# Turning keys and probabilities in 32x32 blocks on VectorE instead of on TensorE, in a decode step of attention and a gated feed-forward

## The chip, the cores and the metric

The kernel runs on one core of one Trainium2 chip. The metric is the device time of one execution in microseconds (us), as the median of several runs. The core has a matrix engine (TensorE, PE in the profile, with its weight loads as PEld), a vector engine (VectorE, DVE), an activation engine (ScalarE, ACT), GpSimd (POOL) and SyncE (SP), which here only issues transfers. Each engine takes its instructions in the order of its own list and waits at semaphores for the others. Sixteen DMA engines move data between the off-chip memory and the on-chip memory of 128 partitions (SBUF). TensorE writes into PSUM, eight banks of 2 KB per partition.

## The reference

One token of a decode step for a batch of 8. A normalised x goes two ways: through grouped-query attention over the last 2048 entries of a key and value cache (32 query heads, 8 key heads, 128 wide), and through a gated feed-forward. The results are multiplied and added to x.

```python
xn = _layernorm(x)                                        # 8 x 512
q  = (xn @ wq) as 8 x 32 heads x 128                      # wq 512 x 4096
k, v = the last W = 2048 rows of the caches, 8 heads, each used by 4 query heads
p  = softmax(q k^T * 128 ** -0.5);  o = p v
s  = o as 8 x 4096 @ wo                                   # wo 4096 x 512
g  = silu((sigmoid(xn @ w_gate) * (xn @ w_up)) @ w_down)  # 512 x 1792, 1792 x 512
out = x + s * g
```

All data are bf16. The caches that are read are 8 batches x 8 heads x 2048 x 128 for keys and as much for values, 67 MB; the weights are another 14 MB.

## The kernel before

**Storage and transfers.** One tile `ring` holds nine slots of 16 KB per partition. A cache tile is one slot: four key heads of one batch, so that partition 4p + l holds 64 consecutive cache rows of head l of the four (`G` = 4, 32 partitions for each head). A batch has two key tiles and two value tiles (`i` = 0, 1). The list `todo` fixes the order of all loads: gate and up weights, the plain part of w_down, a slot for its gathered part, wq, then the keys of tile n with the values of tile n - 3, and wo at the end in four pieces. `pump` issues the next load of the list on SP's queue as soon as the list's head finds a free slot (L172 for cache tiles, L123 for weights); `free` gives a slot back after the last instruction that reads it. The slot of a key tile is given back in `k_transposes`, that of a value tile in `value`.

**The gather.** Of w_down, the first `m0` rows come by an indirect DMA from POOL's queue (L239): 64 partitions each get `SF` rows in one piece, the others none. `SEGS` lists which partitions these are; a selection matrix `sel` on TensorE spreads the matching part of the hidden vector to the same partitions. The remaining rows come as one plain load of `MT` rows per partition.

**Head.** Layer norm, gate and up products, transposes of the hidden vector, then the queries (L387): wq is 512 x 4096, four contraction steps by eight column blocks, written four at a time into the four 32-column strips of the array. Two groups of four transposes bring them into `qm_sb`, padded by zeros so that a window of 32 columns puts the four query rows of one head at the right place.

**Attention, per batch.** The code's main loop (from L675 on) runs over batches `b` and sixteen steps. In each step `k_transposes` turns eight blocks of 128 keys x 128 on TensorE through `perm` into PSUM (L484), and VectorE copies the 128x1024 result to SBUF (L489). After two steps `scores` (L502) forms four products of 32 rows x 512 keys, side by side in the array, into one PSUM bank per batch, whose 128 rows are head of the tile x eighth of the batch's keys (tile and quarter) x query. `row_max` takes each row's own maximum (L515) and four exponentials of 32 rows (L522), with the sums. As each row has a maximum of its own, `stat_rows`, `factor` and `spread` work out, in one row of 128 numbers on one partition, what each row must be scaled by. `p_transposes` turns the probabilities on TensorE (L591) and copies them (L596). `value` (L612) multiplies them by the values two batches behind, in 16 steps for each of the two value tiles; `combine` scales on ScalarE (L632), `normalise` and `turn` bring the result into the layout `oP_sb` (L642, L651, L660, L667). Up to batch 4 (`WIDE`) a value product has 64 rows and 512 columns, after that two of 32 rows and 256.

**Tail.** After the last keys the stages of the last batches are written out one by one, with filler products (`keep`) between them, then the output product with wo (`into`, L372, two halves of 64), two vector instructions (L756, L758) and two stores.

The order on each engine is the order of the code: there is no scheduler, and the tables of `tasks` are written out by hand.

Of the kernel before, what the change touches and what calls it, by code (L numbers as in the profile page):

```python
# [10 lines left out]
def kernel(  # L11
# [30 lines left out]
    CH = CU // 2  # L42
    NU = NQ * NJ
    NR = NU * rep
# [18 lines left out]
    ps_t = ctx.enter_context(  # L63
        tc.tile_pool(name="ps_t", bufs=4, space=bass.MemoryType.PSUM)
    )
    ps_s = ctx.enter_context(
        tc.tile_pool(name="ps_s", bufs=2, space=bass.MemoryType.PSUM)
# [68 lines left out]
    MT = 9  # L136
    SF = 10
    NSEL = 64
    SEGS = [(0, 15, 1), (16, 3, 1), (28, 18, 1), (48, 2, 1)]
    SEGS += [(60, 8, 1), (68, 6, 4), (92, 8, 1), (124, 4, 1)]  # L140
# [142 lines left out]
    xnT_sb = work.tile([P, KT, Z], bf16, name="xnT_sb")  # L283
    nc.vector.memzero(xnT_sb[:])
    nc.vector.tensor_copy(out=xnT_sb[:, :, :B], in_=xnT_ps[:])  # L285
# [8 lines left out]
    M0 = Z - rep  # L294
    qm_sb = work.tile([P, B, Hkv, M0 + Z], bf16, name="qm_sb")
    nc.gpsimd.memzero(qm_sb[:])
    p_buf = [work.tile([P, PG, G, CU], bf16, name=f"p_buf{i}") for i in range(2)]
    for t in p_buf:
        nc.gpsimd.memzero(t[:])
# [20 lines left out]
    for k in range(F // FC):  # L320
        g_ps = ps_t.tile([B, FC], f32, name="g_ps", tag="t")
        for kt in range(KT):
            nc.tensor.matmul(  # L323
                g_ps[:],
                lhsT=xnT_sb[:, kt, :B],
# [9 lines left out]
    h_bf = ktpool.tile([P, CU * P], bf16, name="h_bf", tag="kT")  # L335
    for k in range(F // FC):
        u_ps = ps_t.tile([B, FC], f32, name="u_ps", tag="t")
        for kt in range(KT):
            nc.tensor.matmul(  # L339
                u_ps[:],  # L340
                lhsT=xnT_sb[:, kt, :B],
# [40 lines left out]
    q_ps = [ps_t.tile([P, D], f32, name="q_ps", tag="t") for _ in range(2)]  # L382
    for kt in range(KT):
        for e in range(2):
            for g in range(G):
                c0 = (G * e + g) * D
                nc.tensor.matmul(  # L387
                    q_ps[e][Z * g : Z * (g + 1), :],
                    lhsT=xnT_sb[:, kt, :],
                    rhs=weights[("wq_sb", kt)][:, c0 : c0 + D],  # L390
                    start=(kt == 0),
                    stop=(kt == KT - 1),
                    tile_position=(0, Z * g),
                    skip_group_check=True,
                )
    free(rows_of[("wq_sb", 0)])
    spot_ps = ps_t.tile([P, SF, B], f32, name="spot_ps", tag="t")
# [14 lines left out]
    for e in range(2):  # L412
        q_bf = ktpool.tile([P, D], bf16, name="q_bf", tag="kT")
        nc.scalar.mul(out=q_bf[:], in_=q_ps[e][:], mul=scale)
# [187 lines left out]
    def value(b, i, c):  # L602
# [18 lines left out]
        if c == CU - 1:  # L621
            free(v_tiles.pop((b, i)))
# [173 lines left out]
```

## Time and profile before

| | |
|---|---|
| median of 3 runs | 198.41 us (198.28 to 198.48) |
| the profiled execution: its own time, its span | 198.86 us, 197.1 us |
| PE, DVE, ACT, POOL busy | 163.4, 125.7, 40.8, 9.1 us |
| DMA moved | 81.32 MB, mean 413 GB/s |
| DVE copies of turned keys (L489) | 128 x 684 ns = 84.3 us busy |
| PE transposes of keys (L484) | 1024, 73.4 us busy |
| PE score products (L502) | 256, 25.8 us busy |
| PE value products (L612) | 352, 36.6 us busy |
| chain that ended last, by engine | DMA 65%, PE 25%, DVE 5%, ACT 3% |

The span runs from the first to the last instruction; the execution's own time is 1.8 us longer. Busy time is the sum over instructions of an engine; matmuls overlap, so the mean duration of one is longer than its share of the stream. A line of the profile names the source line, the engine, what was written and read, and the count. The row "DMA" of the slices gives in tenths how full the sixteen DMA engines were in each fortieth of the span. A window's line has start and end, its length, the busy time and count of PE, PEld, DVE, ACT and POOL, the granted clock of TensorE as a share, the DMA share and GB/s.

### The profile page before, as it was taken

Reading aid. Unit: us, or ns where it says so; the run is one execution under the profiler, and the core shown is the slowest. Engines: PE = TensorE matmul, PEld = TensorE weight load, DVE = VectorE, ACT = ScalarE, POOL = GpSimd, SP = SyncE. Lnnn points to the kernel's source line nnn. Section 1 sums busy time; section 2 is a strip of 40 time slices with the busy share of each in tenths; the row PEclk is TensorE's granted clock in tenths of the full one; section 3 lists DMA queues with packets and bytes.
Section 4 is the critical chain, followed back from the end, with each engine's and each line's share of the span. In section 5 each row is a group of like instructions: output and inputs, shape, how many; then the busy total and the mean of one; then the engine's idle time right before and its main releaser. Section 6 shows DMA issues by size and latency. Waiting matters only on the chain.

```text
span 197.1 us, 4818 instructions
## 1 busy us (share of the span) xinstructions
PE 163.4 (83%) x2114; PEld 106.8 (54%) x2114; DVE 125.7 (64%) x247; ACT 40.8 (21%) x95; POOL 9.1 (5%) x31
## 2 busy tenths in 40 slices
PE   0029859999699999799979987999799998878883
PEld 0013423876576575456646654665467566655652
DVE  4540401999799796679667966796549878935201
ACT  0053003001701501600160016001600070071000
POOL 7910000000000000000000000000000000000000
PEclk9999966999999999999999999999879999999999
DMA  6999999999999999999999999999999999999990
GB/s 203 438 440 463 416 406 426 436 436 432 424 429 429 422 426 422 439 432 432 426 432 434 426 426 421 429 436 426 419 442 439 426 431 422 426 429 429 420 401 16
DMA packets 6148, 81.32 MB, mean 413 GB/s; under 512 B 808, under 2 KB 816, under 8 KB 1328
## 3 DMA queue, kind: packets, MB, share of 16 engines
q1 hardware_dynamic: 5936, 80.35, 96.0%
q0 software_dynamic: 144, 0.66, 0.8%
q8 instruction: 16, 0.26, 0.5%
q14 instruction: 4, 0.03, 0.0%
q10 hardware_dynamic: 48, 0.01, 0.0%
HBM read 81.67 MB, written 0.01 MB: 414 GB/s over the span
## 4 chain that ended last, share of the span: by engine, by line
DMA 65%; PE 25%; DVE 5%; ACT 3%; issue 1%; SPq 0%; ACTq 0%
DMA ring<-in_A_k_cache_dram 29%; DMA ring<-in_A_v_cache_dram 13%; PE kT_ps L484 13%; DMA ring<-in_A_wq_dram 11%; DMA ring<-in_A_wo_dram 10%; PE s_ps L502 4%; PE o_ps L612 3%; DMA ring<-in_B_w_gate_dram 3%; DVE kT_sb L489 2%; PE q_ps L387 2%; ACT p_buf L522 2%; PE fin_ps L372 1%; PE d_ps L403 1%; DVE pT_sb L596 1%; ACT L522 1%
## 5 line engine op out<-in xcount | busy, mean ns | idle before, releaser
L489 DVE COPY kT_sb<-kT_ps 128x1024 bf16<-128x1024 bf16 x128 | 84.3, 684 | 26.0 <-PE kT_ps L484 21.2
L484 PE MATMUL kT_ps<-perm,ring 128*128 128x128 bf16 x1024 | 73.4, 221 | 2.0 <-DMA ring<-in_A_k_cache_dram 2.0
L484 PEld LDWEIGHTS <-ring 128*128 128x128 bf16 x1024 | 59.5, 99 | 24.6 <-issue 18.3
L612 PE MATMUL o_ps<-ring,pT_sb 128*32 128x256 bf16 (+1 forms) x352 | 36.6, 330 | 6.6 <-DMA ring<-in_A_v_cache_dram 5.6
L502 PE MATMUL s_ps<-kT_sb,qm_sb 128*32 128x512 bf16 x256 | 25.8, 393 | 1.3 <-DVE kT_sb L489 1.1
L522 ACT ACTIVATE p_buf<-s_ps,st 32x512 bf16<-32x512 f32 x32 | 21.7, 679 | 15.5 <-DVE st L515 15.1
L612 PEld LDWEIGHTS <-pT_sb 128*32 128x32 bf16 (+1 forms) x352 | 12.4, 102 | 19.4 <-issue 17.6
L632 ACT ACTIVATE o_sb<-o_ps,fac 128x512 f32<-128x512 f32 (+1 forms) x8 | 4.9, 608 | 60.5 <-PE o_ps L612 60.5
L596 DVE COPY pT_sb<-pT_ps 128x1024 bf16<-128x1024 bf16 x16 | 10.8, 676 | 1.8 <-PE pT_ps L591 1.8
L502 PEld LDWEIGHTS <-qm_sb 128*32 128x32 bf16 x256 | 7.0, 93 | 8.1 <-issue 1.5
L591 PE MATMUL pT_ps<-turn_rows,p_buf 128*128 128x128 bf16 x128 | 10.7, 227 | 0.0
L591 PEld LDWEIGHTS <-p_buf 128*128 128x128 bf16 x128 | 9.4, 148 | 0.2 <-issue 0.2
L278 PE MATMUL xnT_ps<-ident,xn_bf 8*128 8x8 bf16 x4 | 0.3, 174 | 9.9 <-DVE xn_bf L267 9.9
L549 ACT ACTIVATE w_row<-w 1x128 f32<-1x128 f32 x8 | 2.5, 308 | 28.6 <-DVE w L542 28.6
L346 DVE TENSOR_TENSOR h_bf<-sig,u_ps 8x448 bf16<-8x448 f32 x4 | 2.4, 608 | 6.6 <-PE u_ps L339 6.1
L422 DVE COPY qm_sb<-qT_ps 128x128 bf16<-128x128 bf16 x2 | 1.4, 876 | 8.1 <-PE qT_ps L417 8.1
L323 PE MATMUL g_ps<-ring,xnT_sb 128*8 128x448 bf16 x16 | 5.7, 541 | 0.3 <-DVE xnT_sb L285 0.3
L522 ACT ACTIVATION_READ_ACCUMULATOR p_buf<-s_ps,st 32x1 f32 x32 | 5.9, 184 | 0.0
L515 DVE TENSOR_REDUCE st<-s_ps 128x1 f32<-128x512 f32 x8 | 5.5, 682 | 0.5 <-PE s_ps L502 0.5
L278 PEld LDWEIGHTS <-xn_bf 8*128 8x128 bf16 x4 | 0.2, 114 | 10.0 <-DVE xn_bf L267 10.0
L387 PE MATMUL q_ps<-ring,xnT_sb 128*32 128x512 bf16 x32 | 3.6, 629 | 2.4 <-DMA ring<-in_A_wq_dram 2.4
L642 PE MATMUL m_ps<-ident_f,o_sb 128*128 128x32 f32 x40 | 5.2, 272 | 0.0
(97 smaller groups left out, 97.0 us busy)
## 6 DMA issues: line engine op xcount, KB each, us to landing
ring<-in_A_k_cache_dram SPq DMA_DIRECT2D x16, 2048.0 KB, 28.5
ring<-in_A_v_cache_dram SPq DMA_DIRECT2D x16, 2048.0 KB, 30.4
ring<-in_A_wq_dram SPq DMA_DIRECT2D x1, 4096.0 KB, 21.6
ring<-in_A_wo_dram SPq DMA_DIRECT2D x1, 2048.0 KB
ring<-in_B_w_gate_dram SPq DMA_DIRECT2D x2, 896.0 KB, 6.0
ring<-in_B_w_up_dram SPq DMA_DIRECT2D x1, 1792.0 KB, 13.1
ring<-in_A_wo_dram SPq DMA_DIRECT2D x1, 1280.0 KB
ring<-in_B_w_down_dram SPq DMA_DIRECT2D x1, 1152.0 KB
```

Source lines behind the costliest of these rows:

```text
L323: nc.tensor.matmul(g_ps[:], lhsT=xnT_sb[:, kt, :B], rhs=weights[("wg_sb", kt)][:, k * FC : (k + 1) * FC], start=(kt == 0), stop=(kt == KT ...
L387: nc.tensor.matmul(q_ps[e][Z * g : Z * (g + 1), :], lhsT=xnT_sb[:, kt, :], rhs=weights[("wq_sb", kt)][:, c0 : c0 + D], start=(kt == 0), st ...
L484: nc.tensor.transpose(out=kT_ps[:, c, :], in_=k_sb[:, j * CU + h * CH + c, :], identity=perm[:],)
L489: nc.vector.tensor_copy(out=kT[(b, u)][:, h * CH : (h + 1) * CH, :], in_=kT_ps[:])
L502: nc.tensor.matmul(s_ps[b][NR * l : NR * (l + 1), :], lhsT=qm_sb[:, b, i * G + l, o : o + Z], rhs=t[:, :, PG * l : PG * (l + 1)], start=(u ...
L515: nc.vector.tensor_reduce(out=st[b][:], in_=s_ps[b][:], axis=AX.X, op=ALU.max, negate=True)
L522: nc.scalar.activation(out=p_buf[b % 2][rows, :, l, :], in_=s[rows, :].rearrange("k (c p) -> k p c", p=PG), func=AF.Exp, bias=st[b][rows, ...
L591: nc.tensor.transpose(out=pT_ps[:, c, :], in_=p_buf[b % 2][:, :, :, h * CH + c].rearrange("k p l -> k (p l)"), identity=turn_rows[:],)
L596: nc.vector.tensor_copy(out=pT[b][:, h * CH : (h + 1) * CH, :], in_=pT_ps[:])
L612: nc.tensor.matmul(o_ps[r] if b < WIDE else o_ps[r, 0:2], lhsT=pT[b][:, c, r], rhs=x, start=(c == 0), stop=(c == CU - 1), tile_position=(0 ...
L632: nc.scalar.activation(out=o[:, :n], in_=o_ps[:, :n], func=AF.Copy, scale=fac.pop(b)[:])
L642: nc.tensor.matmul(oT_ps, lhsT=o[:, e, :], rhs=sel[:, e], start=(e == 0), stop=(e == n - 1),)
```

## The change

The transposes of keys and probabilities leave TensorE. VectorE turns a key tile in place, eight steps per batch: the tile is read as 4-byte words (pairs of bf16), and each block of 32 partitions x 32 words is turned by itself. Afterwards the 32 partitions of block a hold pairs of head dimensions, and along each of them stand the 32 former partitions of that block, eight groups of cache rows of four heads each. So `scores` now contracts over all 128 partitions, with queries of all four heads that are zero outside the 32 partitions of one block (`q_wide`, filled for the next batch by four POOL copies in `widen`): four products of 512 columns (two halves of the head, two members of a pair) add up in one PSUM bank. Its rows are block x step parity x 16 queries, two steps share a bank, and a product of `of_row` with `other` puts -1e30 at the places where a query meets another head's keys. A batch has four score banks of 128 rows x 512.

The maxima are taken over both halves and across rows before the exponentials (`row_max`, `both_max`, `turn_max`, `spread_max`), so all rows of a query share one maximum, and the row-by-row scaling goes. These stages of batch b - 1 stand ahead of the first key turn of batch b. The probabilities are turned by one VectorE instruction per batch (`p_turn`), in two halves for the last batch. The value products are 16 steps of 64 rows x 512 columns for every batch but the last, paced over the steps by `PACE`. The queries are formed in one bank of 128 rows per key tile, by 32 products that are no longer side by side.

The gather fetches 64 pieces of 8 rows instead of 10, to other partitions; the plain load has 10 rows per partition instead of 9.

```diff
+    NL = G * rep
+    NE = 4
+    NW = NQ * NE
+    M0 = NL
-        tc.tile_pool(name="ps_t", bufs=4, space=bass.MemoryType.PSUM)
-        tc.tile_pool(name="ps_s", bufs=2, space=bass.MemoryType.PSUM)
+        tc.tile_pool(name="ps_s", bufs=6, space=bass.MemoryType.PSUM)
...
-    MT = 9
-    SF = 10
+    MT = 10
+    SF = 8
     NSEL = 64
-    SEGS = [(0, 15, 1), (16, 3, 1), (28, 18, 1), (48, 2, 1)]
-    SEGS += [(60, 8, 1), (68, 6, 4), (92, 8, 1), (124, 4, 1)]
+    SEGS = [(0, 22, 1), (24, 2, 1), (28, 6, 1), (36, 2, 1), (40, 2, 1)]
+    SEGS += [(60, 2, 1), (64, 7, 1), (72, 2, 1), (76, 3, 1), (80, 3, 1)]
+    SEGS += [(84, 2, 1), (88, 3, 1), (92, 6, 1), (124, 2, 1)]
...
+    for i in range(NQ):
         q_bf = ktpool.tile([P, D], bf16, name="q_bf", tag="kT")
-        nc.scalar.mul(out=q_bf[:], in_=q_ps[e][:], mul=scale)
...
+        nc.scalar.mul(out=q_bf[:], in_=q_ps[i][:], mul=scale)
+        qT = ktpool.tile([P, rep, 2, Z, 2], bf16, name="qT", tag="kT")
+        nc.vector.transpose(
+            out=qT[:].rearrange("p r j z e -> p (r j z e)").bitcast(f32),
+            in_=q_bf[:].bitcast(f32),
+        )
+        for j in range(2):
+            nc.gpsimd.tensor_copy(
+                out=qc[:, :, i, j].rearrange("p b e l r -> p b e r l"),
+                in_=qT[:, :, j].rearrange("p r (l b) e -> p b e r l", b=B),
+            )
...
+    def k_turn(b, s):
+        i, j = s // NJ, s % NJ
+        x = (
+            k_tiles[(b, i)][0][:, j * CU : (j + 1) * CU, :]
+            .rearrange("p c d -> p (c d)")
+            .bitcast(f32)
+        )
+        nc.vector.transpose(out=x, in_=x)
+
+    def scores(b, s):
+        i, j = s // NJ, s % NJ
+        if j % 2 == 0:
+            s_ps[(b, s // 2)] = ps_s.tile([P, CU, Z], f32, name="s_ps", tag="s")
+            nc.tensor.matmul(
+                s_ps[(b, s // 2)][:],
+                lhsT=of_row[:].rearrange("k y l r -> k (y l r)"),
+                rhs=other[:],
+                start=True,
+                stop=False,
+            )
...
+        for n in range(NE):
+            o = (i * NE + n) * P + M0 - NL * (j % 2)
+            nc.tensor.matmul(
+                s_ps[(b, s // 2)][:],
+                lhsT=q_wide[b % 2][:, o : o + P],
+                rhs=k[:, n // 2, n % 2],
+                start=False,
+                stop=(j % 2 == 1 and n == NE - 1),
+            )
+        if j == NJ - 1:
+            free(k_tiles.pop((b, i)))
...
+    def p_turn(b, m0=0, m1=NBK):
+        if m0 == 0:
+            pT[b] = ppool.tile([P, NBK, CU // 2, Z, 2], bf16, name="pT_sb")
+        nc.vector.transpose(
+            out=pT[b][:, m0:m1].rearrange("p m c x e -> p (m c x e)").bitcast(f32),
+            in_=p_buf[b][:, m0:m1].rearrange("k m c x e -> k (m c x e)").bitcast(f32),
+        )
...
+    PACE = (0, 0, 1, 3, 5, 9, 10, 11, 12)
...
+            if s == 0 and b >= 1:
+                scores(b - 1, NT - 1)
+                row_max(b - 1, NBK - 1)
+                both_max(b - 1)
+                if b >= 3:
+                    values(b - 3, PACE[NT], NN - 2)
+                turn_max(b - 1)
+                if b >= 3:
+                    values(b - 3, NN - 2, NN)
+                    combine(b - 3)
+                spread_max(b - 1)
+                exps(b - 1)
+            k_turn(b, s)
+            if s >= 1:
+                scores(b, s - 1)
+                if b >= 2:
+                    pace(b - 2, s)
+            if s % 2 == 1 and s >= 3:
+                row_max(b, s // 2 - 1)
+            if s == 3 and b >= 3:
+                normalise(b - 3)
+            if s == 3 and b + 1 < B:
+                widen(b + 1)
+            if s == 5 and b >= 3:
+                turn(b - 3)
+            if s == 4 and b >= 1:
+                p_turn(b - 1)
+            if s == 5 and b >= 1:
+                factor(b - 1)
```

## The prediction

> **What bounds the kernel now.** I read the slices and queues of the page first, then the issues and the queue's own waits.
>
> ```profile
> DMA  6999999999999999999999999999999999999990
> q1 hardware_dynamic: 5936, 80.35, 96.0%
> q0 software_dynamic: 144, 0.66, 0.8%
> q8 instruction: 16, 0.26, 0.5%
> ring<-in_A_k_cache_dram SPq DMA_DIRECT2D x16, 2048.0 KB, 28.5
> ring<-in_B_w_down_dram SPq DMA_DIRECT2D x1, 1152.0 KB
> SPq L172 <- PE kT_ps L484: 105.9, 23, 8.4
> ```
>
> The reader sees DMA engines that are full in every slice, and a queue (SP's) that stands waiting for a free slot for 105.9 us without emptying them: a cache tile lands 28.5 us after its issue. A stretch in mid-kernel moved 431 GB/s, so a tile of 2.10 MB takes 4.87 us, and 28.5 / 4.87 = 5.8 tiles are under way at any time. A batch (two key and two value tiles) is 19.5 us of transfer. The fetched instructions (q8) share the same 16 engines. Next the chain of waits and the windows at the end.
>
> ```profile
> 171.83 19.82 DMA ring<-in_A_wo_dram
> 191.65 0.04 issue
> 191.69 2.24 PE fin_ps L372 x64
> 193.93 0.02 issue
> 193.96 0.29 DVE prod L756
> ...
> 191.00:191.50 0.50, 0.42 (x3) 0.09 (x1) 0.00 (x0) 0.00 (x0) 0.00 (x0) 1.00 1.03 401
> 191.50:192.00 0.50, 0.31 (x12) 0.31 (x13) 0.00 (x0) 0.00 (x0) 0.00 (x0) 1.00 0.80 311
> 192.00:192.50 0.50, 0.50 (x26) 0.50 (x22) 0.00 (x0) 0.00 (x0) 0.00 (x0) 1.00 0.44 168
> 192.50:193.00 0.50, 0.50 (x22) 0.44 (x18) 0.00 (x0) 0.00 (x0) 0.00 (x0) 1.00 0.13 49
> 193.00:193.50 0.50, 0.50 (x16) 0.39 (x16) 0.00 (x0) 0.00 (x0) 0.00 (x0) 1.00 0.01 4
> ```
>
> In the windows the column before the last is the DMA share: the 16 engines do not end together. From 191.5 on they still do 0.5 x (0.80 + 0.44 + 0.13 + 0.01) = 0.69 us each on the mean, so an even dealing would end at 192.2; the last two (0.13 x 16 = 2.1) end near 193.1. So the end is set by the most loaded DMA engine, then by half of the last product and the store, and compute matters only where it is late for a slot or for the tail.
>
> **The change part by part.** The sum is made against the profiled execution: span 197.1, its own time 198.86, which is 0.45 above the median of 198.41.
>
> *Instructions.* q8's 0.26 MB is 62 bytes for each of the 4228 PE rows (2114 products and as many weight loads), and no other engine has over 250: the fetches are PE's. In the built programs PE's list falls from 4116 to 1732 entries, so 16 fetches become 16 x 1732 / 4116 = 7. One costs 0.5% x 16 x 197.1 / 16 = 0.99 us of one engine (0.89 to 1.08 by the rounding). Nine fewer: 8.9 us, or **-0.56 us** per engine. If the fetches were another engine's the saving is nothing, and the rows exclude a loss.
>
> *Gather and the rows that are loaded plainly.* q0's 0.8% is 25 us for 64 rows of 10 KB, 0.39 us a row. Now 64 rows of 8 KB: 0.31 each, 20 us. The plain part of w_down grows from 1152 to 1280 KB: 0.13 MB / 431 GB/s = +0.30 us on each engine; the gather gives -0.32. Together nothing.
>
> *Dealing.* [...] It can gain between 0.9 (even) and nothing, or lose some tenths if the fetches land elsewhere; I take **-0.55**, a third left.
>
> *DVE.* Gone: 128 copies of 0.684, 16 of 0.676, the one-row arithmetic. New per batch: eight turns of a 128x1024 f32 block and one for the probabilities, four maxima instead of one. No turn is in the trace. From below: the copy of the same bytes, 0.61 back to back. From above: the block goes through the engine twice at one element per cycle. The rate of one element comes from two reductions out of PSUM,
>
> ```profile
> L515 DVE TENSOR_REDUCE st<-s_ps 128x1 f32<-128x512 f32 x8 | 5.5, 682 | 0.5 <-PE s_ps L502 0.5
> L538 DVE TENSOR_REDUCE top<-m_ps 1x32 f32<-1x128 f32 x8 | 2.2, 271 | 2.7 <-PE m_ps L535 2.7
> ```
>
> (682 - 271) / 384 = 1.07 ns an element and 0.13 fixed: 1.23 us once, 2.33 twice. I take 1.2, the row of the same element count per cycle. [...] Per batch: 9 x 1.2 + 4 x 0.68 + 2.0 for the small rows (0.14 to 0.3 each) = 15.5. Waits in DVE's own queue: the last maximum waits for the last scores (1.1), two round trips to PE for the maxima (0.5 each) stand in front of the next keys' first turn, `normalise` costs 0.9: together 3.0. So 18.5 against 19.5: hidden, with 1.0 to spare per batch. The price if that cover goes is the first rival.
>
> *PE.* Gone: 1024 + 128 transposes (84 us). New: 288 score products of 512 columns. One pass of 512 took 3.60 / 8 = 0.45 us for the four-wide query groups at a granted clock of 0.50, so 0.22 at 1.0. Per batch 36 x 0.22 = 7.9, value pairs 16 x 0.28 = 4.4, small products 1.7: 14 of 19.5. The keys are now read at every second element; the strided weight load of p_buf (148 against 99 ns) bounds that at 1.5 times, +3.6, still hidden.
>
> *Head.* The query product is no longer four at a time: 32 passes. They begin at 27.6 with the clock at half (0.50 until 31.2, about 1.0 from 32.5): 11 passes cold, 21 warm, end near 37 instead of 31.2. Then the chain scale, turn, POOL copies (four of some 0.5, four of 0.3), constants on DVE: first scores near 43 instead of 36.7. The next key and value tiles were issued by 22.5 and land until 32.5 + 4 x 4.87 = 52, and the slots of wq come free at 37, so the queue never empties. Cost nothing; the 6 us of lag are worked off at 1.0 per batch. The extra POOL copies before the gather (14 small ones instead of 8, 0.19 each) move its issue by 1.1 us; its rows are wanted 20 us later.
>
> *POOL, ACT, SP.* Four small copies per batch widen the next queries, 1.2 us on an engine that idles, some 15 us ahead of use. Four exponentials stay four (0.68 + 0.18). SP's issues are the same 44; a key tile is freed one score group later, against 5.8 tiles in stock.
>
> *Tail.* The last keys landed at 164.0. From there four turns, the probabilities' turn and the waits are about 11 us to the bias and 3.5 of exponentials: 178.5, as the last but one value tile lands (178.7). After the last value tile (183.8) the same products run; the output product waited 0.6 and 0.3 us for wo, so it follows the DMA. Nothing.
>
> Sum: -0.56 - 0.55 = -1.1. Profiled 197.75, median **197.3**.
>
> **The rivals.**
>
> 1. *DVE becomes the bound* (the other side). The point: with 1.0 to spare over nine turns, a turn above 1.32 us; the lag that the tail stands is some 5 us. At 1.45 a batch takes 20.8: 8 x 1.3 - 5 = +5, so 202; at 2.33 it takes 28.7: 8 x 9.2 - 5 = +68, near 265. For it: no turn in the trace, and its queue now holds every stage of a batch. Against: the element rate.
> 2. *A cold tail.* PE idles 30% where it was 83% busy. A 2.4 us gap had 0.50 behind it at 27.6, and a stretch at 140 to 150 ran at 0.83. The last values (1.9) and the two halves of the output product (2.0 and 2.2) are 6.1 us; if half of that runs at half the clock it grows by 3, less the 0.9 that the output product stood waiting for wo and the 1.1 of the sum: 198.4 + 1.0 = 199.4. [...] Against: filler products stand in the same places.
> 3. *Hidden anyway*: the fetches are not fewer on the engine that ends last, and the dealing only moves the excess. 198.4.
>
> **How the numbers follow.** 0.2% is 0.4 us, about what a measurement here tells from no change. Forecast 0.66: from 196.4 (-0.56, -0.9 and another 0.5 by the rounding and by uneven fetches) to 198.0. Rival 3: 0.14. Rival 2: 0.10, 198.8 to 200, at 199.4. Rival 1: 0.10, 199 up to 265. Faster 0.66, same 0.14, slower 0.20. The range is 196.3 to 199.5: the forecast's ends may be missed in some of its 0.66, so rival 2 is taken in up to its own figure, and rival 1 is left out.
>
> **What would show it.** Right: q8 with about 7 packets, q0 with 0.52 MB, DMA slices still 9 to the end, the share falling within 1 us near 192, turns at 1.15 to 1.25 us, DVE under 80%, the final product near 190.6. Wrong: a slice of DMA below 9 in mid-kernel, SP no longer waiting for slots, turns above 1.3, the granted clock at half in the last 10 us, or an end as ragged as before.

## The result, and the profile after

The changed kernel takes **210.45 us** (median of four runs, 208.97 to 211.44); the kernel before takes 198.44 (198.28 to 198.69) beside it. The ratio is 1.0598 [1.0530, 1.0665]: 12 us slower, where 1.1 us faster was predicted, and outside the range of 196.3 to 199.5. The profiled execution is the shortest of the four: 208.97, with a span of 207.1 against 197.1.

From the page of the changed kernel, its totals, two rows of the slices and two queues:

```profile
PE 161.4 (78%) x936; PEld 63.5 (31%) x936; DVE 126.8 (61%) x202; ACT 35.8 (17%) x87; POOL 19.0 (9%) x73
PEclk9999759959969859999996999697899999999999
DMA  6999999999999999999999999999999999949600
q0 software_dynamic: 144, 0.52, 0.6%
q8 instruction: 7, 0.11, 0.2%
```

Much of what the prediction named is there: 7 packets of instructions, 0.52 MB gathered, VectorE below 80%. But the DMA engines are no longer full to the end, and the clock row has a 5, 6, 7 or 8 again and again in mid-kernel, where the kernel before has one such place, near 142 us:

```profile
PEclk9999966999999999999999999999879999999999
```

The page's chain reads otherwise than before (DMA 65%, PE 25%, DVE 5%):

```profile
PE 50%; DVE 30%; DMA 12%; issue 3%; POOL 2%; ACT 1%; ACTq 0%; POOLq 0%
```

Compute ends last now. A key tile lands sooner after its issue (28.5 us before), as fewer are under way (16.4 / 4.87 = 3.4 against 5.8, worked out as in the prediction), and SP waits for VectorE's turns instead of PE's transposes:

```profile
ring<-in_A_k_cache_dram SPq DMA_DIRECT2D x16, 2048.0 KB, 16.4
```

```profile
SPq L171 <- DVE ring L507: 72.8, 14, 7.6
```

Its groups and waits, from the page (left number busy time and mean ns of one, right the idle time ahead and what ended it):

```profile
L507 DVE STREAM_TRANSPOSE ring<-ring 128x1024 f32<-128x1024 f32 x64 | 75.1, 1213 | 0.0
L525 PE MATMUL s_ps<-ring,q_wide 128*128 128x512 bf16 x256 | 74.5, 419 | 11.2 <-DVE ring L507 10.4
L686 DVE TENSOR_TENSOR oB<-m_ps,band 128x128 bf16<-128x128 f32 x7 | 2.0, 292 | 14.2 <-PE m_ps L677 14.2
L611 DVE TENSOR_REDUCE fac<-m_ps 64x1 f32<-64x2 f32 x16 | 2.5, 156 | 6.2 <-PE m_ps L601 6.1
```

A turn takes the 1.21 us that were forecast, 1.2. But VectorE stands still for 14.2 us in front of seven `oB`, the vector part of `normalise`: five are in the loop (1.9 in a batch at the full clock, 2.7 behind a half-clock stretch), two in the tail (1.6 and 1.5). It stands 6.1 us in front of the factor, 0.54 in each of the later batches.

Where the time came from is read off the ends of each batch's 32nd score product in the trace:

| last scores of batch, us | 0 | 1 | 2 | 3 | 4 | 5 | 6 | 7 |
|---|---|---|---|---|---|---|---|---|
| before | 46.42 | 61.33 | 77.68 | 97.12 | 116.84 | 136.21 | 156.74 | 173.14 |
| changed | 53.05 | 68.28 | 87.31 | 105.66 | 125.34 | 146.78 | 165.11 | 183.46 |

The changed kernel is 6.6 us late after the first batch, as the prediction's head has it, and 10.3 late after the last. Its batches 1 to 7 take 15.2, 19.0, 18.4, 19.7, 21.4, 18.3 and 18.4 us. The kernel before, whose DMA engines are full, takes (173.14 - 46.42) / 7 = 18.1 on the mean, but not evenly: 14.9 and 16.4 in batches 1 and 2, 19.1 on the mean of the last five. The keys are not late in the changed kernel: by the traces the sixth key tile lands at 65.5 us (66.5 before) and the fourteenth at 143.4 (144.5 before), in both kernels one every 9.7 us, so a batch's two every 19.5. From the last scores to the end of the span are 23.6 us here and 23.9 before, so the 10 us are lost before the tail.

The long batches lie on stretches of half clock: the one of 19.0 us on 71.2 to 78.0, the one of 19.7 on one later stretch and the one of 21.4 on two. The windows of the changed kernel around the last three of these stretches (start and end, length, busy time and count of PE, PEld, DVE, ACT, POOL, granted clock, DMA share, GB/s):

```profile
105.28:108.69 3.41, 2.21 (x13) 0.61 (x12) 2.25 (x6) 1.16 (x3) 1.15 (x4) 1.00 1.01 432
108.69:112.11 3.42, 2.96 (x8) 0.80 (x8) 3.42 (x4) 2.21 (x8) 0.00 (x0) 0.50 1.01 431
125.76:129.17 3.41, 1.75 (x11) 0.66 (x10) 2.67 (x7) 1.90 (x5) 0.86 (x3) 1.00 1.04 447
129.17:132.59 3.42, 3.42 (x10) 0.70 (x7) 2.99 (x3) 1.47 (x6) 0.00 (x0) 0.50 0.97 414
139.41:142.83 3.42, 2.26 (x12) 0.93 (x11) 2.83 (x8) 0.00 (x0) 0.00 (x0) 1.00 0.94 402
142.83:146.24 3.41, 3.30 (x9) 0.90 (x9) 1.87 (x3) 0.00 (x0) 0.00 (x0) 0.50 1.04 447
```

In the trace of every run the granted clock is 1.00 or 0.50 for whole stretches of 3.41 us, as in these windows. One at the full clock in which PE was busy for 1.75 to 2.26 us stands ahead of each half-clock one here.

A whole batch that met no half-clock stretch, batch 3, has both engines idle for some 3 to 4 of its 18.35 us:

```profile
87.31:105.66 18.35, 15.43 (x83) 5.69 (x85) 14.52 (x22) 3.37 (x9) 1.15 (x4) 1.00 1.01 430
```

And the middle of batch 4, in the chain of waits of the changed kernel (start, length, what). The clock is full here, but the batch has a half-clock stretch behind it:

```profile
114.67 0.55 PE o_ps L643 x4
115.22 1.02 PE m_ps L677 x8
116.27 0.29 DVE oB L686
116.56 1.15 DVE ring L507
117.71 1.13 DVE pT_sb L593
118.84 1.13 DVE ring L507
119.96 0.58 DVE st L540
120.54 0.21 DVE oP_sb L702
120.89 0.37 PE m_ps L601 x2
121.44 0.17 DVE fac L611
121.80 1.15 DVE ring L507
123.00 1.03 PE s_ps L525 x4
```

VectorE's list puts `oB` ahead of the fifth key turn, so the turns of this batch wait until PE has done the scores and values queued in front of the eight fp32 products of `normalise` (L677). Then VectorE works without a break from 116.27 to 120.75, PE waits for it, and the factor (L601, L611) makes a further round trip ahead of the seventh turn. Neither engine is hidden behind the other.

**Theories.** A: VectorE's list (the round trips of `normalise` and the factor that stand in front of key turns) makes a batch too long to work the head's lag off (the expectations below set it against the mean of 18.1 us). B: half-clock stretches make the batches long. C: it is the round trips for the maxima, ahead of the first key turn. D: the head's 6 us are the loss. The expectations of the first four runs call A, C and D together the LAG theory and B the CLOCK theory; their DMA theory (slots and the dealing set the end) has the landings and the chain above against it.

### The profile page after: what moved, and what is told of

It reads as the page before. It is cut to its first block, busy times and chain, and to the rows that moved or that the text cites. A ratio compares the mean times of both kernels' runs of the same rounds, so it can differ in the third digit from the quotient of the medians.

```text
span 207.1 us, 2435 instructions
## 1 busy us (share of the span) xinstructions
PE 161.4 (78%) x936; PEld 63.5 (31%) x936; DVE 126.8 (61%) x202; ACT 35.8 (17%) x87; POOL 19.0 (9%) x73
## 4 chain that ended last, share of the span: by engine, by line
PE 50%; DVE 30%; DMA 12%; issue 3%; POOL 2%; ACT 1%; ACTq 0%; POOLq 0%
PE s_ps L525 23%; DVE ring L507 17%; PE o_ps L643 11%; DMA ring<-in_A_wq_dram 10%; DVE st L540 4%; PE q_ps L387 4%; PE m_ps L677 3%; DVE pT_sb L593 3%; DMA ring<-in_B_w_gate_dram 2%; PE fin_ps L372 2%; PE s_ps L513 2%; POOL qc L420 1%; DVE fac L611 1%; PE m_ps L601 1%; DVE low L557 1%
## 5 line engine op out<-in xcount | busy, mean ns | idle before, releaser
L525 PE MATMUL s_ps<-ring,q_wide 128*128 128x512 bf16 x256 | 74.5, 419 | 11.2 <-DVE ring L507 10.4
L507 DVE STREAM_TRANSPOSE ring<-ring 128x1024 f32<-128x1024 f32 x64 | 75.1, 1213 | 0.0
L643 PE MATMUL o_ps<-ring,pT_sb 128*64 128x512 bf16 (+1 forms) x288 | 40.4, 375 | 0.4 <-ACT o_sb L664 0.4
L525 PEld LDWEIGHTS <-q_wide 128*128 128x128 bf16 x256 | 23.8, 106 | 45.1 <-issue 30.3
L540 DVE TENSOR_REDUCE st<-s_ps 128x1 f32<-128x512 f32 x32 | 21.7, 677 | 9.0 <-PE s_ps L525 8.7
L582 ACT ACTIVATE p_buf<-s_ps,bias 128x512 bf16<-128x512 f32 x32 | 21.5, 689 | 27.4 <-DVE bias L578 27.4
L643 PEld LDWEIGHTS <-pT_sb 128*64 128x64 bf16 (+1 forms) x288 | 13.2, 106 | 27.6 <-issue 23.9
L428 POOL COPY q_wide<-qc 32x128 bf16<-32x128 bf16 x32 | 9.2, 287 | 98.1 <-PE s_ps L525 96.6
L513 PE MATMUL s_ps<-other,of_row 4*128 4x512 bf16 x32 | 13.1, 409 | 1.5 <-POOL of_row L462 1.5
L686 DVE TENSOR_TENSOR oB<-m_ps,band 128x128 bf16<-128x128 f32 x7 | 2.0, 292 | 14.2 <-PE m_ps L677 14.2
L593 DVE STREAM_TRANSPOSE pT_sb<-p_buf 128x1024 f32<-128x1024 f32 (+1 forms) x9 | 9.8, 1091 | 0.0
L677 PEld LDWEIGHTS m_ps<-ident_f,o_sb 128*128 128x128 f32 x56 | 6.8, 191 | 2.7 <-issue 2.7
L677 PE MATMUL m_ps<-ident_f,o_sb 128*128 128x32 f32 x56 | 7.6, 279 | 0.0
L601 PE MATMUL m_ps<-sums,spread_f 128*128 128x4 f32 x16 | 2.8, 247 | 5.3 <-DVE oP_sb L702 5.3
L611 DVE TENSOR_REDUCE fac<-m_ps 64x1 f32<-64x2 f32 x16 | 2.5, 156 | 6.2 <-PE m_ps L601 6.1
## 6 DMA issues: line engine op xcount, KB each, us to landing
ring<-in_A_k_cache_dram SPq DMA_DIRECT2D x16, 2048.0 KB, 16.4
```

What stands on the lines that cost most here:

```text
L428: nc.gpsimd.tensor_copy(out=q_wide[b % 2][g, : NW * P].rearrange("p (x c) -> p x c", x=NW)[:, :, M0 + Z * a : M0 + Z * a + NL], in_=qc[g, ...
L507: nc.vector.transpose(out=x, in_=x)
L513: nc.tensor.matmul(s_ps[(b, s // 2)][:], lhsT=of_row[:].rearrange("k y l r -> k (y l r)"), rhs=other[:], start=True, stop=False,)
L525: nc.tensor.matmul(s_ps[(b, s // 2)][:], lhsT=q_wide[b % 2][:, o : o + P], rhs=k[:, n // 2, n % 2], start=False, stop=(j % 2 == 1 and n == ...
L540: nc.vector.tensor_reduce(out=st[b][:, m // 2, m % 2 : m % 2 + 1], in_=s_ps[(b, m)][:].rearrange("k c x -> k (c x)"), axis=AX.X, op=ALU.max,)
L582: nc.scalar.activation(out=p_buf[b][:, m], in_=s_ps.pop((b, m))[:].rearrange("k (c e) x -> k c x e", e=2), func=AF.Exp, bias=bias[:, m // ...
```

## The experiments

### The maxima, and the head

The first run takes two key turns out from behind the maxima:

```diff
             if s == 0 and b >= 1:
+                k_turn(b, 0)
                 scores(b - 1, NT - 1)
                 row_max(b - 1, NBK - 1)
                 both_max(b - 1)
+                k_turn(b, 1)
...
-            k_turn(b, s)
+            if s >= 2 or b == 0:
+                k_turn(b, s)
```

> Undoes 'maxima ahead of the next keys' turn': the next batch's first key turn stands ahead of the last maximum, the second between both_max and the cross-row round trip. LAG theory: DVE's waits for the last scores (1.2 per batch) and the two round trips (0.75) are covered by turns: 1.5 to 2 us per batch over 7 batches, 197.5 to 200.5, then the transfers are the bound again. CLOCK theory: PE no longer waits 1.2 us for the first turn, so the granted clock should rise over 0.95 and the gain comes from there; the warm batches stay at 18.3 each. DMA theory: no change.

Measured: 208.46 us, ratio 1.0489 [1.0441, 1.0537], where 197.5 to 200.5 was expected if these waits are the loss. Its undisturbed batch is 18.24, 0.1 less. From its waits:

```profile
DVE oB L686 <- PE m_ps L677: 17.7, 7, 3.6
```

The time that VectorE no longer spent on the maxima it spent in front of `oB` (17.7 instead of 14.2 us in all). In a batch at the full clock its waits for the last scores and the maxima fall from 1.25 to 0.4 us, and the one for `oB` rises from 1.89 to 2.71. C falls.

The second run makes the constants (`own` to `sel_n`) ahead of the gate's products and turns the first three key steps ahead of the queries:

```diff
+    for s in range(NJ - 1):
+        k_turn(0, s)
+
     qc = work.tile([P, B, NQ, 2, 2, G, rep], bf16, name="qc")
...
-            k_turn(b, s)
+            if b > 0 or s >= NJ - 1:
+                k_turn(b, s)
```

> The constants for the scores (own, spread_f, of_row, other, sel_n) are built while DVE and POOL idle before wq lands, and the first three key turns stand ahead of the queries' turn on DVE. LAG theory (the batches start 6.6 us later than before and the cycle of a batch never works it off, the last 20.5 us follow the last scores): first scores near 40.6 instead of 42.4, batch 0 ends 2 to 3 us earlier, and the whole of it arrives at the end: 207.5 to 208.5 against 210.5. CLOCK theory (the loss is PE at half clock at the batches' starts): the head is not it, 209.5 to 211. DMA theory (slots and the dealing set the end): 210 to 211.

Measured: 209.93 us, ratio 1.0487 [1.0415, 1.0560]. The first batch's scores ended 1.36 us earlier (51.69; 2 to 3 were expected), and batches 2 to 7 took 18.96, 19.88, 18.34, 19.93, 21.46 and 19.74: more of them on half-clock stretches. An undisturbed one took 18.34 as before. What the head gained, the clock took; this alone said nothing on D.

### VectorE's list

The vector part of `normalise` goes behind the fifth key turn and the probabilities' turn; the copy of the turned context and the factor's product go one step later, the factor's vector part two.

```diff
             if s == 3 and b >= 3:
-                normalise(b - 3)
+                transposed(b - 3)
...
-            if s == 5 and b >= 3:
-                turn(b - 3)
             if s == 4 and b >= 1:
                 p_turn(b - 1)
-            if s == 5 and b >= 1:
-                factor(b - 1)
+            if s == 4 and b >= 3:
+                banded(b - 3)
+            if s == 5 and b >= 3:
+                turn_a(b - 3)
+            if s == 6 and b >= 3:
+                turn_b(b - 3)
+            if s == 6 and b >= 1:
+                factor_a(b - 1)
+            if s == 7 and b >= 1:
+                factor_b(b - 1)
```

(`transposed` and `banded` are the two halves of `normalise`, `_a` and `_b` PE's part and the vector part of `turn` and `factor`; the arithmetic is the same.)

> The vector part of normalise stands behind key turn 4 and the probabilities' turn, turn's copy and the factors one or two steps later, so DVE does not wait for these products (oB 2.0 us per batch in five batches, factors 0.9 in seven). LAG theory: 10 to 16 us of DVE waits go, of which PE's own 14 to 16 us per batch lets through about 1 us per batch: 202 to 206. CLOCK theory: 208 to 211, as the idle time at the batch boundary stays. DMA theory: no change.

Measured: **197.83 us** (197.63 to 198.08, six runs), ratio 0.9966 [0.9954, 0.9979]: faster than the kernel before. Its last scores are 53.20, 68.57, 87.35, 104.34, 121.31, 138.29, 155.26, 172.25: from batch 3 on a batch takes 16.97 to 16.99 us, every one. The head's lag of 6.8 us behind the kernel before has grown to 9.7 after batch 2, and is then worked off at 19.1 - 17.0 = 2.1 per batch, to 0.9 ahead after batch 7. None of the three theories had this time; the nearest expectation was 202 to 206. The page's rows, one of its batches, its chain and its windows at the end:

```profile
PEclk9999859966985975999999999999999999999999
DMA  6999999999999999999999999999999999999990
104.34:121.31 16.97, 15.31 (x83) 5.62 (x85) 14.25 (x22) 3.36 (x9) 1.15 (x4) 1.00 1.01 431
PE 69%; DMA 13%; DVE 11%; POOL 2%; issue 2%; ACT 1%; ACTq 0%; POOLq 0%
```

```profile
191.00:191.50 0.50, 0.50 (x26) 0.50 (x21) 0.00 (x0) 0.00 (x0) 0.00 (x0) 1.00 0.69 270
191.50:192.00 0.50, 0.50 (x21) 0.43 (x15) 0.00 (x0) 0.00 (x0) 0.00 (x0) 1.00 0.22 82
192.00:192.50 0.50, 0.50 (x19) 0.48 (x16) 0.00 (x0) 0.00 (x0) 0.00 (x0) 1.00 0.03 12
```

The DMA engines are full to the end again and finish near 192.2, where the kernel before had a share of 0.44 in the last of these windows and 0.13 in the next. The span is 0.9 us shorter than before's. The chain is still PE's: compute and the DMA end almost level here. From the last scores to the end are 24.0 us instead of 23.6, as the second half of the output product, which the last pieces of wo feed, takes 2.3 us instead of 1.9.

But this run also had no half-clock stretch after 78 us, so it can't say how much is the list and how much the clock. Two further runs made each half of it by itself. The first moves `oB` only:

```diff
             if s == 3 and b >= 3:
-                normalise(b - 3)
+                transposed(b - 3)
...
             if s == 4 and b >= 1:
                 p_turn(b - 1)
+            if s == 4 and b >= 3:
+                banded(b - 3)
```

> Half of the run that moved both parts: only normalise's vector part (oB) goes behind the fifth key turn and the probabilities' turn; the factor and the turn of the context stay where the changed kernel has them. Theory (DVE stands still for the fp32 products of normalise): DVE waited 14.2 us for them over 7 batches, 2.0 each, against 6.1 for the factor's, so most of the 1.38 us that the undisturbed batch lost (18.35 to 16.97) is here: a batch of 17.2 to 17.6, below the keys' 18.1, and a time of 198 to 201. Rival (PE's order around the factor, whose product stands behind the copy of the turned context and holds the scores behind it): this half gives a few tenths, the batch stays above 18.0 and the time above 205.

The second moves the turn's copy and the factor only:

```diff
-            if s == 5 and b >= 3:
-                turn(b - 3)
             if s == 4 and b >= 1:
                 p_turn(b - 1)
-            if s == 5 and b >= 1:
-                factor(b - 1)
+            if s == 5 and b >= 3:
+                turn_a(b - 3)
+            if s == 6 and b >= 3:
+                turn_b(b - 3)
+            if s == 6 and b >= 1:
+                factor_a(b - 1)
+            if s == 7 and b >= 1:
+                factor_b(b - 1)
```

> The other half: normalise stays whole at its place, the copy of the turned context goes to the next step, the factor's product too, and its vector part one step later. Theory: a batch of 17.8 to 18.2, near the keys' 18.1, so the lag neither grows much nor shrinks, and cold windows remain: 203 to 208. Rival (PE's order around the factor): the batch falls to 17.3 or less and the time to 198 to 200.

Measured: 202.89 us for the first (202.30 to 204.56; undisturbed batch 17.78) and 204.81 for the second (202.10 to 206.46; batch 17.98). From the waits of the first and of the second:

```profile
DVE oP_sb L719 <- PE m_ps L710: 8.8, 7, 1.6
DVE fac L617 <- PE m_ps L605: 5.4, 7, 1.6
```

```profile
DVE oB L697 <- PE m_ps L687: 13.3, 7, 2.7
```

The halves give 0.57 and 0.37 us of a batch, together 0.94, and both at once 1.38. With `oB` moved, VectorE waits for PE one instruction later (at the turned context, 8.8 us over seven batches); with the factor moved it still waits for `oB`. So neither half alone is the cause; one list has several round trips in front of key turns, and what VectorE no longer waits for at one, it waits for at the next. The expectation for the first half, 17.2 to 17.6, was too hopeful.

The last run on the list asks who sets the 16.97. It turns the probabilities a second time, into a tile that nothing reads:

```diff
+        if m1 == NBK and b < B - 1:
+            spare = ppool.tile([P, NBK, CU // 2, Z, 2], bf16, name="spare")
+            nc.vector.transpose(
+                out=spare[:].rearrange("p m c x e -> p (m c x e)").bitcast(f32),
+                in_=p_buf[b][:].rearrange("k m c x e -> k (m c x e)").bitcast(f32),
+            )
```

> The run with both vector parts late, with a second turn of the probabilities into a tile that nothing reads: 1.13 us more on DVE in each of seven batches. It measures what a microsecond of DVE costs there. Theory (DVE's queue sets the batch): 16.97 becomes 18.1, the keys' own period, so the lag of the head is never worked off; last scores near 180, time 204 to 205. Rival (the batch is now set by PE, and DVE's waits for scores, up to 2.1 us a batch, take it in): a batch of at most 17.5 and 198 to 200.

Measured: 200.24 us, ratio 1.0079 [1.0013, 1.0145]. An undisturbed batch is 17.12, only 0.15 longer for 1.13 us more on VectorE. The rival was right on the batch (its time, 198 to 200, was just missed): with the list in this order a batch is set by PE's work (15.3 us busy of 16.97, above) and the round trips for the maxima, and VectorE's waits for scores take the turn in. The time is still 2.4 us more: batch 3 took 18.52 instead of 16.99, with a half-clock stretch at 91.1 that the run without the extra turn had not, and the last scores (174.10) came after 172.6, up to which the DMA ends last (196.2 - 23.6).

### The clock

The mask product that opens a bank was given five times instead of once at the start of a batch, in the 1.16 us in which PE waits for the first turned keys:

```diff
+            fills = 4 if s == 0 and b > 0 else 0
+            for r in range(fills + 1):
+                nc.tensor.matmul(
+                    s_ps[(b, s // 2)][:],
+                    lhsT=of_row[:].rearrange("k y l r -> k (y l r)"),
+                    rhs=other[:],
+                    start=True,
+                    stop=(r < fills),
+                )
```

> The mask product of a batch's first bank is issued five times instead of once, where PE waits 1.2 us for the first key turn: no other change. CLOCK theory: the granted clock rises from 0.92 to over 0.96 and nearly all of the 12 us go, 199 to 201. LAG theory: of the 12 us the clock has some 5 (a warm batch takes 18.35, the cold ones 19.0, 19.7 and 21.4): 204 to 206 if the fillers keep the clock, 210 if they do not. DMA theory: no change.

Measured: 210.32 us, ratio 1.0598 [1.0563, 1.0633]. The batches and the half-clock stretches are those of the changed kernel to 0.02 us, though PE counts as busier ahead of them. The first two windows of the list above, in this run:

```profile
105.28:108.69 3.41, 2.91 (x17) 0.81 (x15) 2.26 (x6) 1.17 (x3) 1.15 (x4) 1.00 0.95 404
108.69:112.11 3.42, 3.13 (x9) 0.90 (x9) 3.42 (x4) 2.19 (x8) 0.00 (x0) 0.50 1.04 446
```

These products contract over four rows of mostly zeros. The next run has full ones at the same place:

```diff
             s_ps[(b, s // 2)] = ps_s.tile([P, CU, Z], f32, name="s_ps", tag="s")
+            for _ in range(4 if s == 0 and b > 0 else 0):
+                nc.tensor.matmul(
+                    s_ps[(b, s // 2)][:],
+                    lhsT=ident[:],
+                    rhs=qc[:].rearrange("p b i j e l r -> p (b i j e l r)")[:, :512],
+                    start=True,
+                    stop=True,
+                )
```

> The changed kernel with four products of full height (128 contraction rows) in front of each batch's first scores, in the gap of 1.14 us in which PE waits for the first turned keys, where the run with four-row products did nothing to the clock. Over all runs so far a stretch of 3.41 us in which PE was busy under 0.53 was always followed by half the clock, and none over 0.66 was, but for stretches that were filled with four-row products. Theory (four rows don't count, full products do): the half-clock stretches at 108.7, 129.2 and 142.8 go, the batches there fall from 19.7 and 21.4 to 18.35 or a little more, last scores near 179, time 205 to 207. Rival (products that compute nothing new don't hold the clock, or the gap is not what the clock looks at): the same stretches and 210 again.

Measured: **202.13 us** (201.67 to 202.62), ratio 1.0163 [1.0111, 1.0214], and this clock row:

```profile
PEclk9999859957999799999999999999999999999999
```

After 70 us there is no half-clock stretch. From batch 3 on a batch takes 18.34 to 18.36, every one, and the last scores end at 177.21. So B is 8.3 us of the 12: 28 products that compute nothing take the time from 210.45 to 202.13. (The profiled execution of the changed kernel was its shortest; between the two profiles the difference is 6.3.) It was more than expected (205 to 207); one reason in the trace is that the half-clock stretches around 57 to 78 us shrank as well. A window like the first of those above, here:

```profile
102.33:105.74 3.41, 2.92 (x17) 0.84 (x16) 2.24 (x6) 0.06 (x1) 1.16 (x4) 1.00 0.99 418
105.74:109.15 3.41, 3.29 (x15) 1.27 (x16) 3.22 (x4) 3.31 (x9) 0.00 (x0) 1.00 1.03 442
```

2.92 us of PE in the window ahead, as with the four-row products, and the clock stays. The two kinds of filler differ in height and in data; which of the two counts was not told apart.

### What is left with the clock held

202.13 is still 3.6 us more than before. Its lag behind the kernel before is 7.0 us after batch 0, 7.8 after batch 2 and 4.1 at the end: batches 3 to 7 work some of it off, at 19.1 - 18.35 per batch, but not enough. If compute sets every batch, a microsecond of the head is still carried to the end one for one. A run with the full products and the earlier head of the second experiment:

> Full-height products in front of each batch's first scores, and besides the earlier head (constants early, the first three key turns ahead of the queries' turn), which by itself brought the first batch's scores 1.36 us forward and nothing in the time. Theory (with the clock held, a batch costs 18.35 against the keys' 18.1, so a lag of the head is carried to the end one for one): batches of 18.35 from the third on, last scores 1.2 to 1.6 us earlier than with the full products alone (177.2), span 199.2 to 199.6, time 200.5 to 201.0. Rival (the lag is worked off on the way, or the head's gain is lost in the first batches): 201.7 to 202.6 as with the full products alone.

Measured: 199.31, 200.13, 204.88 and 205.12 us, median 202.50. The four split by the clock: the two short runs have a mean granted clock of 0.963 and 0.964 (0.957 with the full products alone), the two long ones 0.941, and the profile is of a long one. The two short ones are 2.0 to 2.8 below 202.13, more than the 1.1 to 1.6 expected. In the profiled one the steps can be added up against the run with full products alone: batch 0 ends 1.88 earlier (51.55), batches 1 and 2 together take 2.54 more (half-clock stretches at 54.8, 65.0 and 71.8), four batches of 18.34 to 18.36 change nothing, and batch 6 on a half-clock stretch at 157.2 (behind one with PE busy for 2.14 of 3.41 us) takes 1.56 more: 177.21 - 1.88 + 2.54 + 1.56 = 179.43, which is where its last scores are. Where no stretch of half clock intervenes, the batches are as long with the earlier head as without: a microsecond of the head, or of a slow clock, is a microsecond at the end. The stretch at 157.2 shows that the products make the half clock rarer here, not impossible. D holds, but only because A does; in the run with VectorE's list put right the same head lag costs nothing.

The last of this group puts the full products into that run with the list put right:

> The same full products in the run that puts normalise's and the factor's vector parts later. Theory (that run's end is set by the DMA, its clock only matters up to 78 us): the half-clock stretches between 57 and 78 go or shrink, the second batch falls from 18.8 towards 17, last scores 1 to 2 us earlier, but the time stays at 197.5 to 198.0. Rival (its end is still set by compute): 196.5 to 197.2.

Measured: 197.79 us (197.69 to 197.92), ratio 0.9945 [0.9897, 0.9993]. The last scores of batch 2 end at 85.93 instead of 87.35 and those of batch 7 at 172.01 instead of 172.25; the time is the same. There the DMA ends the kernel, and the chain of its page has DMA at 35%.

Both parts late, the earlier head and the first two key turns ahead of the maxima together:

> Both parts late, and besides constants early, the first three key turns ahead of the queries' turn and the first two turns of each batch ahead of the maxima. Theory (a lag is worked off once a batch costs less than 18.1, and then only the DMA ends the kernel): nothing beyond the run with both parts late, 197.5 to 198.0, with last scores earlier by a microsecond or more. Rival (the tail after the last scores still ends last): faster by the 1.4 us that the head gained, up to 196.5.

Measured: 198.18 us (197.87 to 200.21), ratio 0.9988 [0.9958, 1.0019]: nothing gained. Batches fall to 16.4 until VectorE has caught up with the keys and waits for them (13.8 us in all), and the last scores are at 172.77.

### The dealing

The kernel before with the new dealing alone, keeping its 16 fetches (`MT`, `SF` and `SEGS` of the diff above):

> The kernel before with only the new dealing (eight selected rows wide, ten plain tiles, the new groups), with its 16 fetches of instructions. [...] Rival (the dealing by itself is better, fetches or not): 197.7 to 198.2.

Measured: 199.38 us (199.25 to 199.58) against 198.58 beside it, +0.8, where the author's estimate was 0.3 to 0.9 (198.8 to 199.3): it rests on how the gathered rows fall to the DMA engines, which no run shows. The ratio is 1.0025 [0.9976, 1.0074], an interval that one long run of the kernel before (200.78) widens. Its windows at the end are more ragged:

```profile
191.50:192.00 0.50, 0.43 (x3) 0.09 (x1) 0.00 (x0) 0.00 (x0) 0.00 (x0) 1.00 0.62 238
192.00:192.50 0.50, 0.30 (x12) 0.29 (x13) 0.00 (x0) 0.00 (x0) 0.00 (x0) 1.00 0.42 168
192.50:193.00 0.50, 0.50 (x26) 0.50 (x21) 0.00 (x0) 0.00 (x0) 0.00 (x0) 1.00 0.36 139
193.00:193.50 0.50, 0.50 (x22) 0.43 (x18) 0.00 (x0) 0.00 (x0) 0.00 (x0) 1.00 0.10 37
```

The DMA shares of these windows in the kernel before are 0.80, 0.44, 0.13 and 0.01: the fall begins earlier here and ends half a microsecond later, as the last half of the output product does (192.20 instead of 191.69).

The run with the list put right, with the old dealing:

> The run with both parts late, but with the dealing of the kernel before (ten selected rows wide, nine plain tiles, the old groups). Compute no longer ends last there, so the DMA engines do, and this is the price of the dealing with 7 fetches. [...] Rival (the dealing only moves the excess, the fewer fetches did all): within 0.2 of 197.8.

Measured: 198.93 us (198.33 to 199.22), ratio 1.0005 [0.9982, 1.0027], so 0.7 to 1.1 more than with the new, where 0.3 to 0.9 (198.1 to 198.7) was estimated in the same way. It is no clean price: wq landed 0.8 us later (the first query product is at 27.40 instead of 26.63), the head was colder (half the clock up to 32.66 us instead of 30.36), the last scores came at 173.80, and compute ended last. What can be said is that with 16 fetches the old dealing is the better; with 7 the new one came out faster, but not by the dealing alone.

## Why the prediction was wrong

*Instructions, gather, dealing.* 7 packets and 0.52 MB are right. The sum of -1.1 was nearly right where compute does not end last: with the list put right the span is 196.2 against 197.1, -0.9, and the medians are lower by 0.6 and, with the full products, 0.8. How it splits into fetches and dealing was not measured. No run shows how the gathered rows fall to the DMA engines, on which the dealing's -0.55 rests; what the runs showed is that the new dealing without the fewer fetches cost 0.8 us, and that the old one with 7 fetches took 198.93 us against 197.83, no clean price.

*DVE.* The turn is right (1.21 against 1.2); with the prediction's 0.13 us fixed it is (1213 - 130) / 1024 = 1.06 ns an element, beside the 1.07 of the reductions. The batch is nearly right too: 18.5 forecast, 18.35 measured at the full clock, though made up a little otherwise: 14.5 busy and 3.8 of waits (87.31 to 105.66), against 15.5 and 3.0. `normalise` alone costs 1.9 of waits in such a batch, and 2.7 behind a half-clock stretch, where 0.9 was put.

*Head: the step that failed.* First scores at 42.4 were forecast as near 43. "Cost nothing; the 6 us of lag are worked off at 1.0 per batch" is the wrong step. It set 18.5 against 19.5 us, the time of four tiles at 431 GB/s, for every batch. But the first four key tiles come without values between them, and the kernel before took only 14.9 and 16.4 us for batches 1 and 2. There the changed kernel could work nothing off:

| last scores behind the kernel before, us | after batch 0 | after batch 2 | after batch 7 |
|---|---|---|---|
| changed | 6.6 | 9.6 | 10.3 |
| with the clock held by full products | 7.0 | 7.8 | 4.1 |
| with VectorE's list put right | 6.8 | 9.7 | -0.9 |

With the clock held, the five batches that follow work off 3.7 us, so 0.7 each against the kernel before; seven at 1.0 were forecast. (The 18.1 us that the expectations call the keys' period is a mean that batches 1 and 2 pull down.) The 4.1 that are left are, less what the tail stands, about the 3.6 us of the 12.

*Tail.* That "the lag that the tail stands is some 5 us" is wrong too: from the last scores to the end of the span are 23.6 us wherever compute ended last, and 23.9 in the kernel before, so it stands 0.3. The forecast ended its sum for the tail at the exponentials and took the products behind them to be those of before; by the chain PE works from the last scores on, and the value products alone are 8.9 of the 23.6 us. The same five microseconds made rival 1 too cheap.

*PE: the term that was left out, and the larger one.* "14 of 19.5" was worked out at a granted clock of 1.0; at that clock a batch keeps PE busy for 15.4 us. The half-clock stretches, which the sum puts at nothing in the batches, are 8.3 us of the 12. (The split into 8.3 and 3.6 is that of this order. The list put right, without a filler, took all 12.6, as the half-clock stretches after 78 us went with it.) The trace of before had one of these stretches in mid-kernel; the prediction saw that PE would idle more, and put a price on it in the tail only (rival 2, where the clock then stayed at 1.0).

*The rivals.* Rival 1 had VectorE as part of the bound, which is behind the 3.6 us, but at the wrong point: its turn above 1.32 us did not come; what came is a tail that stands 0.3 us, so that a VectorE batch of 18.35 shows although it is below 19.5. Rival 2 had the right cause at the wrong place. Neither had a chance above 0.10, and no rival put them together: VectorE's waits thin out PE's work, and the thinner work brings the half clock, which makes the waits longer (1.9 and 2.7 us for `oB`). The full products show that denser work brings the clock back; that VectorE's waits are what thins it is read from PE's share of a batch, 0.84 here and 0.90 with the list put right, and no run isolates it.

## What to carry to other kernels

Add a head's lag up batch by batch against the kernel before, as its trace shows them, instead of one spare time for every turn of the loop: the first turns may work nothing off. When a tail follows, read how much lag it stands from the last input to the end. When work leaves TensorE, look at the granted clock in mid-kernel: in fourteen runs here it stayed full behind all 462 stretches of 3.41 us in which PE was busy for 0.70 or more, and 28 full products in a known gap took 8.3 us off. In an engine's list, an instruction that waits for another engine's round trip belongs behind the work that this engine could do meanwhile; move all such waits together, since one moved by itself hands much of its time to the next (here 0.57 and 0.37 us of a batch were gained by one alone, 1.38 by both).

## What the runs showed of the hardware

In fourteen runs (all but the one with four-row products), of the stretches of 3.41 us at the full clock after 36 us, all 41 in which PE was busy for less than 0.53 were followed by half the clock, and none of the 462 with 0.70 or more; between lie 78, of which 15 were. There the share does not decide: with the list put right, a stretch of 0.64 came in five batches and the clock stayed, and the kernel before fell to half the clock behind one of 0.64 (138.4 us). No gap has to be long for it: in the changed kernel no gap of PE between 45 and 200 us is above 1.2 us, and the clock fell to half five times there.

The products of four rows count as busy in the profile and did not hold the clock: in the run that added them, three stretches with a busy share of 0.73, 0.77 and 0.85 were followed by half the clock, which in the other runs none above 0.67 was. Without the products of four rows, the three shares are 0.40, 0.45 and 0.57, like those of the other runs.

A batch of 16.97 us is nearly five such stretches (17.07), so each batch finds its gap at the same place of a stretch; one of 18.35 does not. This would explain why the run with the list put right kept its clock from 78 us without any filler; it was only argued, not tried.
